# Reordering ScalarE's copies and VectorE's weight conversions in the opening of a delta-rule attention with an MLP

## The chip, the cores and the metric

The kernel runs on one core of one Trainium2 chip. A core has five engines with queues of their own, which work side by side and wait for each other through semaphores: TensorE (PE in the profile) multiplies matrices, VectorE (DVE), ScalarE (ACT) and GpSimd (POOL) work element by element, and SyncE (SP) issues most of the transfers from memory. Each engine takes its own instructions strictly in the order in which the program lists them. The metric is device microseconds for one execution; several executions are timed and their median is given.

## The reference, cut to what matters

Inputs are q, k and v (4 batches, 8 heads, 768 tokens, 48 wide), beta (one number for each token and head), and two weight matrices w_in (384 x 2048) and w_out (2048 x 384). All is float32 or float64 on the host; the weights are stored as float64.

```python
k_n = k / (norm(k) + 1e-6)
state = 0                                    # 48 x 48 for each batch and head
for t in range(S):                           # 768 tokens in order
    y[t]  = q[t] @ state
    v_old = state^T @ k_n[t]
    state = state + beta[t] * outer(k_n[t], v[t] - v_old)
x = y of all heads side by side              # 3072 x 384
h = x @ w_in
out = (h * clip(h + 3, 0, 6) / 6) @ w_out    # 3072 x 384
```

## The kernel before, in words

**Blocks of tokens.** The loop over 768 tokens is done in 24 blocks of 32 tokens, all four batches at once, so that a tile has 128 rows. I call them token blocks 0 to 23. For each block the kernel

- normalizes the keys (`norms`, `prep` at L505: the scaling is L510 on POOL);
- turns keys and queries on PE (`pt`, L524) and copies them with ACT to `KQ` (L532), keys first, then queries;
- multiplies them to scores (`sc`, L547), which DVE masks to `L` and `LB` (L558);
- needs the inverse of a triangular matrix made of `L`. Block 0 has its own product form (`product`, L569). Blocks 1 to 4 go together: `halves_of` (L715) turns `L` with L469, does a forward substitution on two half-size problems with fourteen rounds of two DVE operations (L730, L735), and turns the result back (L473). Then `join` (L666) puts the two halves together for each block, with a transposition (L694), a product on PE (`pi`, L684), an addition and a second transposition (L698, L702), a second product (L684) and a copy by ACT (L710);
- runs the `chain` (L787): read the state (`ks`, L806), form the right-hand side R (L901, L909), multiply by the inverse (`pz`, L827) and copy the result with ACT back to R (L927; for block 0 this is its only R), form the output (`py`, L827, then `y`, by ACT at L861 for block 0), turn it (`yt`, L873), copy it to `xT` (L877, ACT), and update the state (`su` on PE at L938, subtracted by DVE at L956).

**The MLP.** `up` (L982) multiplies a pair of blocks, 256 tokens, by w_in; for the first pair each block goes alone, 128 tokens. PE makes one slice of 128 hidden units at a time (`ph`, L994), ACT a scaled relu of it (L1001), DVE the gated product (L1004). I call a slice a hidden unit. A `ph` needs one of four places in PSUM; each is free again when the gated product, or the copy, that reads it is done. `down` (L1153) multiplies by w_out. From 190 us on, forms with fewer products take over; the change does not touch them.

**The weights.** They come as float64, 16 pieces of 768 KB (weights 0 to 7 are w_in, 8 to 15 w_out), and become float32 on the chip. For a piece, ACT does four steps on the exponents (`scales`, L356) and DVE three on the rest: L378, L383 (both into a buffer `m`), and L389, which multiplies the two parts into the weight's place. The exponents stand in two buffers in turn, so the first L356 of weight i must wait for the L389 of weight i - 2. A piece is loaded into a place that an earlier piece has left (L331): load 11, for example, needs the first L356 and the L383 of weight 6 done. Hidden units 1 and 2 need weight 0, units 3 and 4 weight 1, and so on.

**The order.** For the first part the order is written by hand, as a string of words, `ORDER`. Each word advances one generator by one step, so the string fixes the order in which every engine gets its instructions:

```python
gens.update(
    a=scales(), c=rest, w=pieces(), q=queries(), v=values(), B=betas(), k=keys(), z=settings(), s=more_settings(),
    ua=up(0, 0), ub=up(0, 1), u=mlp_units(),
)
makers = {
    "p": lambda t: prep(t, False), "h": lambda t: chain(t, False), "y": lambda t: outs[t],
    "n": early_norms, "m": mask, "b": scaled, "x": lambda t: product(t) if t < G0 else join(t),
    }
```

So `a` is one exponent step on ACT and `c` one conversion step on DVE; `w`, `q`, `k`, `v` are loads; `p3` is the next step of the preparation of block 3 (its steps: scale keys, turn keys, copy keys, turn queries, copy queries, scores, masks); `h0` the next of block 0's chain (product, R, update on PE, update of the state on DVE); `y0` of its output (product, y, turn, xT); `i1` one step of the substitution of blocks 1 to 4; `x1` one of block 1's join; `ua` one hidden unit of block 0, `ra` its relu, `ga` its gated product. `*n` repeats a word.

Of the kernel before, what the change touches and what calls it, by code (L numbers as in the profile page):

```python
# [22 lines left out]
k*2 B*3 k*2 n0 k*2 z B s*2 n0*6 k*2 q*2 n1 q n1 q w k p0 z*3 k n1*2 k*2 n1*2 z p0*2 s k p0*3 a k a  # L23
m0 a n2 m1 p0 x0*2 w q x0 n1 x0*3 c*2 n2 a k s p1*2 a s*2 k q s*2 x0 n2 k*2 c x0 n2 x0 w q a*4 q p1
n2 k*2 a x0 m2 p1 c*2 p1 n2*3 b1 q b0 s p1 x0 q w x0 n2 q*2 c*3 x0 n4 k p1 k p2*2 x0*2 a*2 c a*2 q*3
a*2 w v p3*2 q x0 q n4 p2*2 c p2 v c n4*2 a*3 z v n4 c a m3 v c p2 n4*2 q p2 k c b2 h0 c h0 w a*2 h0
p4*2 a*2 m4 p3 q*4 h0 q k w p4*2 c*5 v*2 p3 k p3*3 k*2 p4*2 v*2 p4 m6 k a w a w i1*3 k i1*7 a i1*2 a
i1*2 v i1*2 k b3 k y0 c y0*3 ua*2 ra*2 i1*3 w v ga v a*3 i1*2 ua i1 h1 i1 q w ua ra ua i1 ra*2 ga i1
k ua a*2 ra ga i1 ga ua ra ua ra i1 ga i1*4 ua ga n5 x1*2 k x1 c a ra v a*2 ga x2 k*2 ga*2 ua*2 x1
ra*2 x1*2 ua h1*2 n5 k ga c ra ga*2 h1 c y1*2 ua ra w ga ua ra x2 n5 ga y1*2 ua ra ga h1 v*3 n5*2 k  # L30
y1*2 ua a ra x2 ub*2 a n5 rb*2 h1 x3 ga c*2 v W a h2 y2 gb ub rb gb x2 gb ub*2 n5*2 b4 rb n5 x2*2 h2
gb rb gb m5 a n5*2 y2 ub rb gb v c q*2 v q*5 n5 ub n5 rb gb h2 c h2 q ub y2 h2 y2 rb ub p5 b5 rb
gb*2 a*2 x3 p5 ub y2*2 k p5*2 h2 rb h3 p5 gb h3 ub*2 q rb gb rb gb ub a x3 p6 v c x4 x3 rb gb ub p7
rb gb y3 c*2 v c p7*2 y3 v p7*2 b6 x3 q x3 ub p6 h3 a p6 c p5*2 rb gb k m7 w p6 h3 u p6 k*2 q*3 a*2
y3 a p6 c y3 v y3*2 u n9 v k q a c a c*2 u*2 ru gu w k a*2 c a*2 x4 c*2 ru p7 a gu k u a*2 p7 p6 m8
u*3 a k u*2 k h3 w ru*2 a*2 gu*2 x4 c*2 x4 k c*2 a p8 k a*2 u ru k h3 u*2 h4 ru a b8 gu k gu y4 p8*3
u h4 k*2 c q k*9 q u p8*2 x4 k ru k*2 gu k c n9 q u q*2 p8 k*2 b7 n9*2 i2 u x4 q i2*2 q ub ru gu u
rb gb i2*2 h4*2 u*2 i2 ru i2*6 y4 i2 gu i2*7 u i2 ru gu i2 u*3 ru i2*4 gu ru i2*2 v i2 c gu u*3 a u
ru c i2 u*2 i2 gu i2*3 q i2*5 y4 h4 n9 i2 e*2 n9*2 i2*4 q i2 y4 e n9 u ru i2*3 u i2 ru*2 gu h4 u n9
i2*2 u i2 e i2*6 y4 u k n9*3 u gu i2 y4 n9 i2 p9 q i2*2 gu  # L40
"""


# [1521 lines left out]
```

## Time and profile before

| | us |
|---|---|
| median of 3 timed runs | 663.66 (663.46 to 663.9) |
| profiled execution, its own time | 662.06 |
| span of the profiled execution | 660.3 |
| PE busy | 632.5 (96%) |
| DVE busy | 499.2 (76%) |
| ACT busy | 282.3 (43%) |
| POOL busy | 225.1 (34%) |
| PE busy in 0 to 20, 20 to 40, 40 to 60 | 7.67, 13.26, 15.57 of 20 each |

The span is what the profile covers, from the first to the last instruction; the time of the execution is a little longer. The profile gives each instruction's start and length, and in brackets how long its engine had been idle before it and which instruction let it go. Lines of the timeline put together instructions of one kind that follow each other closely ("x64"). A busy PE need not be a PE at its peak, because ends of matmuls are modelled. The granted clock (PEclk) is the share of TensorE's full clock that it was given.

### The profile page before, as it was taken

The numbers are of one execution on the slowest core, as the hardware profiler recorded it, in microseconds if no ns is written. First come the engines' busy times: TensorE is split into PE (matmuls) and PEld (weight loads), VectorE is DVE, ScalarE is ACT, GpSimd is POOL, SyncE is SP. The second block draws the span as 40 slices with busy tenths as digits, with TensorE's granted clock in tenths as the row PEclk, the third lists the DMA queues.
The fourth block names the chain that finished last, engine by engine and source line by source line (L and its number), as shares of the span: only waits on it lengthen the run. The fifth ranks groups of instructions, "written<-read, shape, count | busy, mean of one in ns | idle before, by whom it ended". The sixth has DMA issues, their size and how long they took to land.

```text
span 660.3 us, 26640 instructions
## 1 busy us (share of the span) xinstructions
PE 632.5 (96%) x11640; PEld 569.2 (86%) x11640; DVE 499.2 (76%) x1170; ACT 282.3 (43%) x548; POOL 225.1 (34%) x352
## 2 busy tenths in 40 slices
PE   2768999999999999999999999999999999999997
PEld 2658987776689989999999999999999999999997
DVE  5899877798657988758988848979658998456354
ACT  5887689332243154154154244244244144153250
POOL 6531022003661353553254354164051242331430
PEclk9998999999999999999999999999999999999999
DMA  7888346202040030041030030020020020000000
GB/s 174 204 198 235 77 102 164 51 25 43 9 87 18 3 74 3 3 90 22 3 74 3 2 74 3 2 63 2 3 50 2 3 49 3 23 18 2 26 1 24
DMA packets 88692, 33.28 MB, mean 50 GB/s; under 512 B 80224, under 2 KB 83424, under 8 KB 88576
## 3 DMA queue, kind: packets, MB, share of 16 engines
q1 hardware_dynamic: 88224, 31.29, 20.8%
q8 instruction: 91, 1.49, 0.9%
q10 hardware_dynamic: 352, 0.30, 0.2%
q14 instruction: 25, 0.20, 0.1%
HBM read 26.84 MB, written 4.72 MB: 48 GB/s over the span
## 4 chain that ended last, share of the span: by engine, by line
PE 91%; DVE 3%; DMA 2%; SPq 1%; ACT 1%; issue 1%; DVEq 0%
PE po L1226 28%; PE ph L1066 27%; PE ph L994 9%; PE po L1162 6%; PE ks L806 4%; PE su L938 3%; PE pt L524 3%; PE pz L827 3%; PE py L827 3%; PE sc L547 2%; PE yt L873 1%; DMA spare<-in_moe_w_in_dram 1%; PE pi L684 1%; DMA w_out<-in_moe_w_in_dram 1%; SPq L168 1%
## 5 line engine op out<-in xcount | busy, mean ns | idle before, releaser
L1066 PE MATMUL ph<-xT,w_in 128*128 128x128 f32 (+1 forms) x720 | 156.8, 321 | 0.0
L1030 POOL TENSOR_TENSOR g<-g 128x256 f32<-128x256 f32 (+1 forms) x144 | 88.6, 616 | 104.7 <-ACT g L1080 99.1
L1066 PEld LDWEIGHTS ph<-xT,w_in 128*128 128x128 f32 x720 | 116.8, 191 | 6.7
L1226 PE MATMUL po<-w_out,g 128*128 128x192 f32 x640 | 110.6, 326 | 0.0
L1226 PEld LDWEIGHTS po<-w_out,g 128*128 128x128 f32 x640 | 104.6, 190 | 0.5
L1080 ACT ACTIVATE g<-ph 128x512 f32<-128x512 f32 x72 | 43.1, 598 | 105.1 <-PE ph L1066 105.1
L1226 PE MATMUL po<-spare,g 128*128 128x192 f32 x480 | 86.7, 332 | 0.0
L1226 PEld LDWEIGHTS po<-spare,g 128*128 128x128 f32 x480 | 77.2, 190 | 1.8
L994 PE MATMUL ph<-xT,w_in 128*128 128x128 f32 (+1 forms) x384 | 72.0, 338 | 0.6 <-ACT xT L877 0.6
L1236 POOL TENSOR_TENSOR o<-o,u 128x192 f32<-128x192 f32 x18 | 13.3, 739 | 163.8 <-ACT o L1233 86.6
L994 PEld LDWEIGHTS ph<-xT,w_in 128*128 128x128 f32 x384 | 59.6, 195 | 7.7 <-ACT xT L877 0.8
L1093 DVE TENSOR_TENSOR g<-ph,g 128x256 f32<-128x256 f32 x72 | 30.2, 419 | 46.8 <-PE ph L1066 33.5
L759 DVE TENSOR_TENSOR pr<-A 128x30 f32<-128x30 f32 (+9 forms) x150 | 57.3, 382 | 3.3
L1212 DVE TENSOR_TENSOR g<-g 128x512 f32<-128x512 f32 x80 | 56.1, 722 | 3.5 <-PE po L1226 3.5
L1113 DVE SCALAR_TENSOR_TENSOR g<-o,g 128x512 f32<-128x512 f32 x72 | 52.6, 730 | 7.8 <-ACT o L1110 7.7
L764 DVE TENSOR_TENSOR A<-A,pr 128x30 f32<-128x30 f32 (+9 forms) x150 | 55.1, 367 | 3.3
L1110 ACT ACTIVATE o<-g,halves 128x512 f32<-128x512 f32 x72 | 52.2, 725 | 11.3 <-DVE g L1113 8.4
L1066 PE MATMUL ph<-beta_tok,sums_in 128*128 128x128 f32 x288 | 55.9, 275 | 0.0
L356 ACT ACTIVATE spare<-spare,places 128x768 uint16<-128x768 uint16 (+1 forms) x56 | 52.8, 947 | 3.2 <-DMA kf<-in_k_dram 1.6
L1233 ACT ACTIVATE o<-po 128x192 f32<-128x192 f32 x40 | 13.3, 332 | 82.7 <-PE po L1226 79.2
L510 POOL TENSOR_TENSOR kb<-kf,inv 128x384 f32<-128x384 f32 x24 | 21.7, 907 | 75.5 <-issue 43.1
L1162 PE MATMUL po<-w_out,g 128*128 128x384 f32 x128 | 45.4, 490 | 0.0
(141 smaller groups left out, 1019.1 us busy)
## 6 DMA issues: line engine op xcount, KB each, us to landing
kf<-in_k_dram SPq DMA_DIRECT2D x96, 48.0 KB, 2.6
qb<-in_q_dram SPq DMA_DIRECT2D x96, 48.0 KB, 2.4
vf<-in_v_dram SPq DMA_DIRECT2D x96, 48.0 KB, 2.1
out_dram<-o SPq DMA_DIRECT2D x90, 48.0 KB, 1.6
spare<-in_moe_w_in_dram SPq DMA_DIRECT2D x4, 768.0 KB, 6.6
w_out<-in_moe_w_in_dram SPq DMA_DIRECT2D x4, 768.0 KB, 6.1
w_out<-in_moe_w_out_dram SPq DMA_DIRECT2D x4, 768.0 KB, 5.8
spare<-in_moe_w_out_dram SPq DMA_DIRECT2D x4, 768.0 KB, 5.2
```

The source lines that it names most:

```text
L356: nc.scalar.activation(out=z, in_=z if n else d.bitcast(I16)[:, :, :, 3], func=func, bias=places[:, n : n + 1], scale=scale,)
L759: nc.vector.tensor_tensor(out=pv, in0=A[:, j + 1 :, j].unsqueeze(2).to_broadcast([n, w, j]), in1=A[:, j, 0:j].unsqueeze(1).to_broadcast([n ...
L764: nc.vector.tensor_tensor(out=A[:, j + 1 :, 0:j], in0=A[:, j + 1 :, 0:j], in1=pv, op=ALU.subtract)
L994: nc.tensor.matmul(ph[:, cols], lhsT=w_in[:, s, f * 128 : (f + 1) * 128], rhs=xT[:, s, cols], start=(s == 0), stop=(s == NKT - 1),)
L1030: nc.gpsimd.tensor_tensor(out=out, in0=a, in1=b, op=op)
L1066: nc.tensor.matmul(ph[:, n], lhsT=w, rhs=x, start=start, stop=stop, skip_group_check=True)
L1080: nc.scalar.activation(out=gt, in_=ph[:], func=ACTF.Copy)
L1110: nc.scalar.activation(out=r, in_=g, func=ACTF.Relu, bias=half, scale=1.0 / 6.0)
L1113: nc.vector.scalar_tensor_tensor(out=g, in0=r, scalar=1.0, in1=g, op0=ALU.min, op1=ALU.mult)
L1162: nc.tensor.matmul(pos[c][:], lhsT=gs[blk, f // 2][:, f % 2, c * P : (c + 1) * P], rhs=w_out[:, f, :], start=(f == 0), stop=(f == NFC - 1),)
L1212: nc.vector.tensor_tensor(out=A(f, *out, 4), in0=A(f, *a, 4), in1=A(f, *b, 4), op=op)
L1226: nc.tensor.matmul(ps[n][:], lhsT=A(f - f % 2, *a)[:, f % 2], rhs=b[:, f], start=(f == 0), stop=(f == HF - 1),)
```

## The change

Only the string `ORDER` differs. No instruction is added, removed or resized; some stand at other places in their engine's queue. The diff rewraps many lines. This is what is left when both strings are written out (the rest is the same):

```diff
 ... c p2*2 v c n4*2
-a*3 z v n4 c a m3 v c p2 n4*2 q p2 k c b2 h0 c h0 w a*2 h0 p4*2 a*2 m4
-p3 q*4 h0 q k w p4*2 c*5 v*2 p3 k p3*3 k*2 p4*2 v*2 p4 m6 k
-a w a w i1*3 k i1*7 a i1*2 a i1*2 v i1*2 k b3 k y0 c y0*3 ua*2
+a*2 z v n4 c m3 v c p2 n4*2 q p2 k c b2 h0*2 p3 a w p3*2 h0 a h0 p4*2 p3 a m4
+q*4 c p3 q k w p4*2 c p4*2 c v*2 p4 k*3 v*2 a m6 k
+y0 a y0 a*2 w a w i1*3 k i1*7 a i1*2 a i1*2 c v i1*2 k b3 k y0*2 ua*2
 ra*2 i1*3 w v ga v a*3 ...
-k ua a*2 ra ga i1 ...
+k ua a ra ga i1 ...
 ... ua ga n5 x1*2
-k x1 c a ra v a*2 ga x2 ...
+c*2 k x1 c a c a ra v a*2 ga x2 ...
```

Engine by engine, as the two programs list them:

- **ACT.** Before: the four L356 of weight 4, R of block 0 (L927), the four of weight 5, keys of blocks 3 and 4 and queries of blocks 3 and 4 (four L532), the four of weight 6, y (L861), xT (L877). After: two of weight 4, R, keys of block 3, the third, queries of block 3, the fourth, the first of weight 5, keys and queries of block 4, two of weight 5, y, the last of weight 5, the four of weight 6, xT. Later the first L356 of weight 8 goes from ahead of the relus of hidden units 6 to 8 to behind them and behind a square (L407); the relu of unit 9 stays behind it and behind the second L356 of weight 8.
- **DVE.** The last conversion of weight 4 goes behind the two updates of the state (L956). The first two of weight 5 go between the masks of block 3 and those of block 4; its third goes into the substitution, where the third of weight 6 was (one operation earlier). All three of weight 6 go behind the first transposition of block 1's join (L694), ahead of the first conversion of weight 7, of the gated products of units 7 to 9, and of L698 and L702.
- **PE.** The queries of block 3 are turned ahead of the state update of block 0, and the scores of block 3 come ahead of the turning of block 4's queries. The rest stands as before.
- **POOL and SP.** Their orders are the same.

## The prediction

> **What bounds the kernel now.** I read the page first, then busy time by stage, then the timelines of the three engines that the change reorders. The page:
>
> ```profile
> PE   2768999999999999999999999999999999999997
> PEclk9998999999999999999999999999999999999999
> ...
> PE 91%; DVE 3%; DMA 2%; SPq 1%; ACT 1%; issue 1%; DVEq 0%
> ```
>
> The chain that ended last is TensorE (PE) for 91%. In order of time nearly all its other pieces lie before 61.24 us. The stages agree:
>
> ```profile
> 40.00:60.00 20.00, 15.57 (x362) 14.15 (x354) 18.53 (x49) 16.46 (x26) 3.59 (x7) 0.91 0.89 246
> 60.00:80.00 20.00, 19.06 (x670) 17.49 (x669) 18.02 (x49) 15.53 (x36) 2.15 (x4) 1.00 0.35 99
> 80.00:100.00 20.00, 20.00 (x663) 17.23 (x663) 14.47 (x34) 15.34 (x30) 6.14 (x8) 1.00 0.45 100
> ```
>
> After the length, each group is an engine's busy time (PE, PEld, DVE, ACT, POOL). PE loses 4.4 us in 40 to 60, 0.94 in 60 to 80, and nothing more until the last slices. So the edit is worth what it moves the moment from which PE never waits again. Now that moment is the first join, at 61.24; the second join product comes at 63.43. PE's work behind it is the same in both versions.
>
> TensorE, start and length in us:
>
> ```profile
> 39.29 1.27 PE L938 MATMUL su<-R,sums_in 32*64 32x48 f32 x61 [1.75 <-ACT R L927]
> 41.31 0.44 PE L938 MATMUL su<-R,sums_in 32*64 32x48 f32 x3 [0.75 <-issue]
> 49.92 0.55 PE L873 MATMUL yt<-ident,y 128*128 128x128 f32 x3 [2.41 <-ACT y L861]
> 51.05 3.55 PE L994 MATMUL ph<-xT,w_in 128*128 128x128 f32 x18 [0.58 <-ACT xT L877]
> 61.24 0.72 PE L684 MATMUL pi<-X,sums_in 16*32 16x16 f32 x64 [0.94 <-DVE sums_in L694]
> ```
>
> ScalarE (ACT); the brackets are what the edit aims at and what it makes late:
>
> ```profile
> 38.77 0.47 ACT L927 ACTIVATE R<-pz 128x384 f32<-128x384 f32 x1
> 44.54 1.09 ACT L532 ACTIVATE KQ<-pt 128x512 f32<-128x512 f32 x2 [0.29 <-PE pt L524]
> 50.51 0.49 ACT L877 ACTIVATE xT<-yt 128x384 f32<-128x384 f32 x1 [0.64 <-PE yt L873]
> 53.35 0.37 ACT L1001 ACTIVATE g<-ph,halves 128x128 f32<-128x128 f32 x1 [0.92 <-PE ph L994]
> 56.46 0.78 ACT L1001 ACTIVATE g<-ph,halves 128x128 f32<-128x128 f32 x2
> ```
>
> VectorE (DVE), substitution start to join:
>
> ```profile
> 47.70 1.93 DVE L469 STREAM_TRANSPOSE A<-L 128x1024 f32<-128x1024 f32 x1
> 57.36 0.28 DVE L1004 SCALAR_TENSOR_TENSOR g<-g,ph 128x128 f32<-128x128 f32 x1
> 58.00 0.28 DVE L1004 SCALAR_TENSOR_TENSOR g<-g,ph 128x128 f32<-128x128 f32 x1
> 60.74 0.45 DVE L694 STREAM_TRANSPOSE sums_in<-X 128x256 f32<-128x256 f32 x1
> 61.11 0.52 DVE L378 TENSOR_SCALAR spare<-spare 128x768 uint32<-128x768 uint32 x1
> 62.54 0.44 DVE L702 STREAM_TRANSPOSE sums_in<-sums_in 128x256 f32<-128x256 f32 x1
> ```
>
> The substitution runs back to back on DVE from 47.70, with gated products (L1004) of the first hidden units between its rounds. The fifth starts at 58.00, 0.09 after its relu on ACT ended (57.91): there is no room for a later relu.
>
> **Step 1, up to the substitution.** Nothing is added or removed; work is reordered. R's copy need not queue behind two exponent steps (0.97 each): the product it reads ends at 37.53, so R runs 37.56 to 38.0 instead of 38.77 to 39.24. The update then runs from about 38.4 (one set of query transposes, 0.95, now stands ahead of it) and, with the same 0.75 issue gap, ends near 40.9 instead of 41.75. Token block 4's key transposes end at 41.9 (4 x 0.24), block 3's scores at 43.0 (1.1, as at 34.92), block 4's query transposes at 43.95; ACT copies them by 44.55; its scores end at 45.4 (0.75, as at 45.19) to 45.8 (1.18, as at 34.92). DVE has by then done two state updates, weight 4's last conversion and two of weight 5's (45.25), so it is not the limit. Two maskings, 0.35 each: the substitution starts at **46.1** instead of 47.70, a gain of 1.6.
>
> **Step 2, what ACT pays.** Between 34.96 and the copy xT, ACT has the same instructions in both (twelve exponent steps, R, four copies of keys and queries, y: about 14.8 us). Before, it idles some 0.8 among them. Now it waits 0.6 for R's product and 1.45 (42.5 to 43.95) for block 4's query transposes. y moves ahead of five exponent steps, but xT stays behind them: it starts at about 51.75, **1.2 later** than 50.51. If those waits vanish it starts at 50.3.
>
> **Step 3, the hidden wait.** PE's first hidden unit follows xT, at 52.3 instead of 51.05. First and second relu start about 53.6 and 54.9 (1.28 a unit, as 52.07 to 53.35); then, as before, three exponent steps of weight 7 (2.9) stand ahead of relus three to five, which end at 58.4, 58.75 and 59.05 (now 56.85, 57.24, 57.91). DVE, started at 46.1, reaches the third L1004 at 46.1 + 9.66 = 55.8 and waits 2.6; the fifth starts at 59.1, not 58.0. The rest (2.74 to L694's start, 0.45 for it) ends at **62.3** instead of 61.2: the gain has become a loss of 1.1.
>
> **Step 4, three conversions behind L694.** Weight 6's L378, L383 and L389 now follow L694, ahead of weight 7's L378, three L1004 and the join's L698 and L702. By 0.6, 1.05 and 0.95 (rows of weight 5, 42.26 to 44.87) that is 2.5 us on the chain to the second product. ACT adds to it: the first exponent step of weight 8 overwrites what weight 6's L389 reads, so it waits for it, and it and one more step (1.03 + 0.84) stand ahead of the ninth relu (0.37), whose L1004 is queued ahead of L698. Counted from L694's end: L389 ends at 2.5, the relu at 4.8, that L1004 at 5.05, L698 at 5.4, L702 at 5.85, PE's second product at **5.9**. Now it is 63.43 - 61.2 = 2.2. So 3.7 more.
>
> Of what is queued behind: on PE two hidden units (they fill 1.5 of the wait) and the product; behind that X's copy and the chain, which keep their distances. SP's and POOL's orders are unchanged, but load 11 (issued at 59.06) waits for weight 6's L383 and goes at about 63.9; behind it are values that now wait until 63.63 for R of the next block, which shifts with the join, and its data are first read at 95.30. That costs nothing; without cover it would be the same 4.8.
>
> **Sum:** 1.1 + 3.7 = **4.8 us**. The profiled execution took 662.06 (span 660.3, 1.76 around it); it would take 666.9. The median of the runs shown is 663.66, 1.6 above; on that I forecast **668.5**.
>
> **The clock.** PE did little from 48 to 51 and was then granted half its clock:
>
> ```profile
> 52.00:54.00 2.00, 2.00 (x12) 2.00 (x11) 1.79 (x8) 1.01 (x3) 0.00 (x0) 0.50 1.08 312
> 56.00:58.00 2.00, 2.00 (x17) 1.96 (x18) 1.89 (x10) 1.64 (x5) 0.00 (x0) 1.00 0.95 349
> ```
>
> The 18 matmuls at 51.05 took 3.55 (18 at 74.28: 2.27), the reading of the state after them 1.44 (73.20: 1.15), so such a stretch costs up to 1.6. The sum keeps this one stretch. In the new order PE is nearly idle again from 61.5 to 65.6, so a second one may follow: a rival below. The Trainium skill ("TensorE: Matmul & The Clock Gate", Part 1) states that the gate judges free-running windows of about 3.4 us and drops to half rate after an idle one. The trace agrees: 0.50 lasted from 52 to about 55.3. By that rule a second stretch is likelier than by this one case alone, which would make it some 670.
>
> **Rivals.**
> - *The waits on ACT close.* If PE runs early at its later pace (four transposes 0.60 at 82.75, 1.11 at 41.68), xT starts at 50.3 and L694 ends between 59.7 (no relu wait) and 61.2. Then -1.5 to 0, plus 3.7: 2.2 to 3.7, **666.6** in the middle. For it: PE has fewer gaps ahead. Against it: its transposes are slow throughout 18 to 44.
> - *The clock falls twice.* The scores and outputs of step 1 stay at the slow pace (0.8 on xT) and a second half-rate stretch follows the join (up to 1.6): 4.8 + 0.8 to 2.4, **670.3**.
> - *Half of it.* No relu wait, and the ninth relu is no wait either: -1.5 + 2.5 = +1.0, **664.7**, within 0.2%.
> - *Faster.* The earlier substitution carries through to the join and the conversions behind L694 fall into slots that nobody waits for: -1.6, **662.1**. It decides from where L702 ends ahead of 63.4; with L694 at 59.7 that leaves 3.7 for a queue that I count at 5.85. I see no row that shortens it so.
> - *It does not do what it says:* block 4's scores wait for its transposes in PE's queue anyway, and the substitution starts at 47.4. L694 is held by the relus, so the sum stays near 4.8; it is part of the forecast.
>
> **How the numbers follow.** Forecast 0.50 (667.6 to 669.6), closed waits 0.20, clock twice 0.16, half 0.08, faster 0.06. A measurement of this kernel tells 0.2% (1.3 us) from no change. Slower 0.86, same 0.08, faster 0.06. The range leaves out "half", "faster" and the ends of the others: 665.5 to 671.0.
>
> **What would show it.** Step 1: L469 starts near 46.1 (47.4 or more: wrong). Step 2: xT starts at 51 to 52. Step 3: a wait of DVE for ACT ahead of the third L1004, some 2 us, and L694 ending after 61.2. Step 4: PE waits twice between the first join product and the second, which starts about 6 us behind L694; ACT waits for DVE ahead of weight 8. Then PE full to the end. The forecast is wrong if PE waits after 75 us in the new kernel, or if the ninth relu does not stand in the join's way.

## The result and the profile after

| | before | after |
|---|---|---|
| median, 6 runs each on one chip (us) | 663.53 (662.48 to 663.9) | 670.19 (667.24 to 674.01) |
| profiled execution, its span (us) | 662.06, 660.3 | 670.92, 669.1 |

The ratio is 1.0105, with a 95% interval of 1.0071 to 1.0139: the change makes the kernel slower by 6.7 us. In the profiled executions it is 8.9 us; of the kernel after that one lies 0.7 above its median, and of the kernel before 1.5 below. The steps below are read in the profiled ones.

The page of the kernel after, where the fourth slice of PE and the granted clock of the third to the fifth are lower than before and nothing later is (the record of the clock of the kernel before begins only at 45 us, in the third slice; see the last section):

```profile
PE   2766999999999999999999999999999999999997
PEclk9967899999999999999999999999999999999999
...
PE 92%; DMA 2%; DVE 1%; SPq 1%; ACT 1%; issue 1%
```

Busy time by stage (length, then PE, PEld, DVE, ACT, POOL, granted clock, DMA share, GB/s):

```profile
40.00:60.00 20.00, 12.74 (x293) 10.72 (x294) 13.75 (x37) 12.90 (x19) 2.29 (x6) 0.57 0.96 237
60.00:80.00 20.00, 16.54 (x451) 15.32 (x454) 15.66 (x39) 11.60 (x26) 2.15 (x4) 0.83 0.24 60
80.00:100.00 20.00, 20.00 (x650) 18.61 (x640) 16.49 (x45) 14.93 (x33) 4.50 (x6) 1.00 0.38 86
```

PE loses 7.3 us in 40 to 60, where it lost 4.4, and 3.5 in 60 to 80, where it lost 0.94. From 80 us on it is full. So the loss lies ahead of the moment from which PE no longer waits; that moment is now the second join product (71.15 us; behind 75 us PE waits only once, for 0.2). PE in the kernel after:

```profile
38.02 1.17 PE L938 MATMUL su<-R,sums_in 32*64 32x48 f32 x57
40.85 0.33 PE L938 MATMUL su<-R,sums_in 32*64 32x48 f32 x7 [1.66 <-issue]
46.34 0.48 PE L547 MATMUL sc<-KQ 64*32 64x64 f32 x17 [0.90 <-issue]
53.83 4.21 PE L994 MATMUL ph<-xT,w_in 128*128 128x128 f32 x18 [4.07 <-ACT xT L877]
65.08 0.73 PE L684 MATMUL pi<-X,sums_in 16*32 16x16 f32 x64 [0.97 <-DVE sums_in L694]
68.30 2.93 PE L994 MATMUL ph<-xT,w_in 128*128 128x128 f32 x12 [2.49 <-DVE g L1004]
71.15 1.05 PE L684 MATMUL pi<-X,sums_in 32*32 32x16 f32 x64
```

"issue" means that PE stood still and no semaphore that the profile shows held it. It did so inside the state update and again inside block 4's scores. The waits for ACT (4.07) and DVE (2.49) are those of the prediction. ACT and DVE:

```profile
37.11 0.49 ACT L927 ACTIVATE R<-pz 128x384 f32<-128x384 f32 x1 [0.97 <-PE pz L827]
48.31 0.49 ACT L861 ACTIVATE y<-py 128x384 f32<-128x384 f32 x1 [2.09 <-PE py L827]
53.31 0.47 ACT L877 ACTIVATE xT<-yt 128x384 f32<-128x384 f32 x1
67.49 1.00 ACT L356 ACTIVATE spare<-w_out,places 128x768 uint16<-128x768 int16 x1 [3.23 <-DVE w_in L389]
69.36 0.35 ACT L1001 ACTIVATE g<-ph,halves 128x128 f32<-128x128 f32 x1
```

```profile
47.66 1.94 DVE L469 STREAM_TRANSPOSE A<-L 128x1024 f32<-128x1024 f32 x1
60.26 0.29 DVE L1004 SCALAR_TENSOR_TENSOR g<-g,ph 128x128 f32<-128x128 f32 x1 [2.41 <-ACT g L1001]
64.59 0.44 DVE L694 STREAM_TRANSPOSE sums_in<-X 128x256 f32<-128x256 f32 x1
66.49 0.96 DVE L389 SCALAR_TENSOR_TENSOR w_in<-spare 128x768 f32<-128x768 f32 x1
70.33 0.45 DVE L702 STREAM_TRANSPOSE sums_in<-sums_in 128x256 f32<-128x256 f32 x1
```

R is 1.66 us earlier than before (37.11, was 38.77), and yet the substitution (L469) starts at 47.66, where it was 47.70. xT is 2.8 later, L694 ends 3.84 later (65.03, was 61.19), and the second product stands 6.12 behind that end, where it was 2.24. From that product to the end of the span it is 597.95 us, where it was 596.9. 3.84 + 3.88 + 1.05 = 8.8, which is the whole difference of the spans.

### The profile page after: what moved, and what is told of

Same layout as the page of the kernel before. It is cut to its first block, busy times and chain, and to the rows that moved or that the text cites. A ratio compares the mean times of both kernels' runs of the same rounds, so it can differ in the third digit from the quotient of the medians.

```text
span 669.1 us, 26639 instructions
## 1 busy us (share of the span) xinstructions
PE 636.4 (95%) x11640; PEld 571.9 (85%) x11640; DVE 499.3 (75%) x1170; ACT 281.2 (42%) x548; POOL 224.0 (33%) x352
## 3 DMA queue, kind: packets, MB, share of 16 engines
q8 instruction: 91, 1.49, 0.9%
## 4 chain that ended last, share of the span: by engine, by line
PE 92%; DMA 2%; DVE 1%; SPq 1%; ACT 1%; issue 1%
PE po L1226 28%; PE ph L1066 27%; PE ph L994 10%; PE po L1162 6%; PE ks L806 4%; PE pt L524 3%; PE py L827 3%; PE pz L827 3%; PE su L938 3%; PE sc L547 3%; PE yt L873 1%; DMA w_out<-in_moe_w_in_dram 1%; SPq L168 1%; DMA spare<-in_moe_w_in_dram 1%; PE pi L684 1%
## 5 line engine op out<-in xcount | busy, mean ns | idle before, releaser
L1066 PE MATMUL ph<-xT,w_in 128*128 128x128 f32 (+1 forms) x720 | 156.8, 321 | 0.0
L1066 PEld LDWEIGHTS ph<-xT,w_in 128*128 128x128 f32 x720 | 116.9, 191 | 6.6
L994 PE MATMUL ph<-xT,w_in 128*128 128x128 f32 (+1 forms) x384 | 74.6, 347 | 6.8 <-ACT xT L877 4.1
L994 PEld LDWEIGHTS ph<-xT,w_in 128*128 128x128 f32 x384 | 61.9, 203 | 14.4 <-ACT xT L877 4.5
L356 ACT ACTIVATE spare<-spare,places 128x768 uint16<-128x768 uint16 (+1 forms) x56 | 52.3, 941 | 2.8 <-DMA kf<-in_k_dram 1.7
L1162 PE MATMUL po<-w_out,g 128*128 128x384 f32 x128 | 45.4, 490 | 0.0
```

Source lines behind the costliest of these rows:

```text
L356: nc.scalar.activation(out=z, in_=z if n else d.bitcast(I16)[:, :, :, 3], func=func, bias=places[:, n : n + 1], scale=scale,)
L994: nc.tensor.matmul(ph[:, cols], lhsT=w_in[:, s, f * 128 : (f + 1) * 128], rhs=xT[:, s, cols], start=(s == 0), stop=(s == NKT - 1),)
L1066: nc.tensor.matmul(ph[:, n], lhsT=w, rhs=x, start=start, stop=stop, skip_group_check=True)
L1162: nc.tensor.matmul(pos[c][:], lhsT=gs[blk, f // 2][:, f % 2, c * P : (c + 1) * P], rhs=w_out[:, f, :], start=(f == 0), stop=(f == NFC - 1),)
```

## The experiments

The edits are given as words of `ORDER` or as lines of code. The table has the profiled execution of each kernel (us; distance: from L694's end to the second join product) and the ratio of its runs to those of the kernel before on the same chip.

| kernel | L469 starts | xT starts | L694 ends | distance | ratio (95%) |
|---|---|---|---|---|---|
| before | 47.70 | 50.51 | 61.19 | 2.24 | |
| after | 47.66 | 53.31 | 65.03 | 6.12 | 1.0105 (1.0071 to 1.0139) |
| after_again | 47.15 | 52.86 | 63.84 | 5.80 | 1.0084 (1.0052 to 1.0116) |
| e1 | 48.90 | 53.97 | 65.04 | 2.44 | 1.0044 (1.002 to 1.0069) |
| e2 | 47.33 | 50.09 | 60.89 | 6.12 | 1.0059 (1.0039 to 1.0079) |
| e3 | 48.08 | 50.22 | 61.91 | 6.14 | 1.006 (1.0037 to 1.0083) |
| e4 | 47.21 | 52.26 | 63.76 | 6.13 | 1.0097 (1.0072 to 1.0122) |
| e5 | 48.05 | 53.69 | 65.44 | 6.13 | 1.0115 (1.0073 to 1.0157) |
| e6 | 48.14 | 53.81 | 63.25 | 5.81 | 1.0228 (1.0192 to 1.0264) |
| e7 | 47.81 | 53.48 | 64.37 | 4.81 | 1.0221 (1.0181 to 1.026) |
| e8 | 48.57 | 50.71 | 64.45 | 3.90 | 1.0027 (1.0009 to 1.0045) |
| e9 | 49.52 | 55.22 | 66.00 | 5.93 | 1.0194 (1.0166 to 1.0221) |
| e10 | 44.44 | 51.38 | 63.18 | 6.13 | 1.019 (1.0142 to 1.0238) |
| e11 | 48.50 | 51.36 | 62.19 | 2.24 | 1.0135 (1.0093 to 1.0178) |

**e1: the three conversions in the substitution instead of behind L694** (the kernel after, changed).

```diff
-k ua a ra ga i1 ...
-c*2 k x1 c a c a ra v a*2 ga x2
+k ua a ra c*3 ga i1 ...
+k x1 a c a ra v a*2 ga x2
```

> The changed kernel with one thing else: weight 6's three conversions stand ahead of the third gated product in the substitution, where VectorE idles 2.4 us in the changed kernel waiting for a relu, and no longer behind L694. My theory (late relus hold L694, and the conversions behind it lengthen the way to the second join product): L694 ends at about the same place as in the changed kernel (65.0, give or take 0.5), ScalarE no longer waits for weight 6 ahead of weight 8, and the second join product starts 2.3 to 2.6 us behind L694's end instead of 6.1; the time falls by 3.5 to 5 us from the changed kernel, to 665 to 667. Rival (the loss is the slow clock and the issue gaps ahead of the substitution, and the order behind L694 matters little): within 1.5 us of the changed kernel.

Measured: the conversions ran while DVE waited for the third relu, L694 ended at 65.04 as in the kernel after, and the second product came 2.44 behind it. PE of e1, with no wait between the two join products:

```profile
65.10 0.73 PE L684 MATMUL pi<-X,sums_in 16*32 16x16 f32 x64 [0.99 <-DVE sums_in L694]
65.75 1.60 PE L994 MATMUL ph<-xT,w_in 128*128 128x128 f32 x12
67.48 0.72 PE L684 MATMUL pi<-X,sums_in 32*32 32x16 f32 x64
```

So the conversions' place is worth 3.7 us here, and DVE's wait was real: three conversions fitted into it at no cost.

**e2: the conversions behind L694 alone** (the kernel before, changed: weight 6's conversions and the first step of weight 8 go where the change has them).

```diff
-... p4 c*5 v*2 p3 ... k y0 c y0*3 ... k ua a*2 ra ga ... x1*2 k x1 c a ra
+... p4 c*3 v*2 p3 ... k y0 y0*3 ... k ua a ra ga ... x1*2 c*2 k x1 c a c a ra
```

> The kernel before with the third part alone: weight 6's three conversions go behind L694, and the first exponent step of weight 8 behind the square, which it has to follow. My theory: substitution starts 0.3 earlier (47.4, the scores of block 4 end at 46.7), but its fifth gated product still waits for a relu that ends at 57.9, so L694 still ends near 61.2; the second join product starts 5.9 us behind it instead of 2.2: 3.7 us slower than before, 667.2, up to 1.6 more if TensorE then gets a second stretch at half clock. Rival (the conversions behind L694 fall into slots that nobody waits for): L694 ends 1.2 to 2.5 earlier and the kernel is faster than before by 1 to 2 us.

Measured: 667.84 us. L694 ended 0.3 earlier, no more; the relus hold it, not by the fifth as I expected but by the third, which DVE waited 0.77 for. The second product came at 67.01, 3.6 later than before. PE of e2:

```profile
64.15 2.93 PE L994 MATMUL ph<-xT,w_in 128*128 128x128 f32 x12 [2.49 <-DVE g L1004]
67.01 0.80 PE L684 MATMUL pi<-X,sums_in 32*32 32x16 f32 x64
```

This part alone makes 3.9 of the 6.7 us. It is the same price as in e1, taken from the other side.

**e3: xT ahead of the exponent steps** (the kernel after, changed).

```diff
-y0 a y0 a*2 w a w i1*3 ... k b3 k y0*2 ua*2
+y0 a y0 a y0*2 a w a w i1*3 ... k b3 k ua*2
```

> The changed kernel with one thing else: block 0's y is turned and copied to xT ahead of weight 6's four exponent steps instead of behind them. My theory: xT starts near 49.8 instead of 53.3, the first relu waits only for the four exponent steps (54), the third ends near 57.5 instead of 60.2, L694 ends at 61 to 62 instead of 65.0, and the way from there to the second join product stays at about 6: 3 to 4 us less than the changed kernel, 666 to 667. Rival (the substitution is late for itself, by the scores that come late): L694 within 1 us of 65.0 and the time within 1 us of the changed kernel.

Measured: xT at 50.22, no wait of 2.4 for the third relu, and L694 ended at 61.91, 3.1 earlier, although the substitution itself started 0.4 later. So xT's place in ACT's queue, through the relus, is what made L694 late. The distance stayed at 6.14, and the time (668.10 us) improved by less than L694 did and less than expected: the granted clock was 0.50 from 64.5 to 74.7 (the 12 matmuls after the second wait took 2.93; from the second product to the end it was 600.65, where the kernel after has 597.95).

**e4: the ninth relu ahead of the first step of weight 8** (the kernel after, changed).

```diff
-c*2 k x1 c a c a ra
+c*2 k x1 c ra a c a
```

> The changed kernel with one thing else: the ninth relu stands ahead of weight 8's first two exponent steps. My theory: VectorE no longer waits 1.3 us for it ahead of L698, and the second join product starts about 4.7 us behind L694's end instead of 6.1; weight 8's steps then stand ahead of X's copy, so that about 1 us is left as a gain. If the 6.1 us come from VectorE's own queue and the clock, nothing changes.

Measured: a miss. The distance stayed at 6.13. L702 ended early, but PE was not ready:

```profile
67.03 2.93 PE L994 MATMUL ph<-xT,w_in 128*128 128x128 f32 x12 [2.49 <-DVE g L1004]
69.89 1.05 PE L684 MATMUL pi<-X,sums_in 32*32 32x16 f32 x64
```

The two hidden units ahead of the product ran at half clock, 2.93 where e1 shows 1.60. They and the ninth relu are two equally long ways.

**e5: the load of weight 6 later** (the kernel after, changed).

```diff
-q*4 c p3 q k w p4*2 c p4*2 c v*2 p4 k*3 v*2 a
+q*4 c p3 q k p4*2 c p4*2 c v*2 p4 k*3 v*2 w a
```

PE's stop inside the update fell where transfers fill the DMA engines; this takes one of them away.

> The changed kernel with one thing else: the load of weight 6 (768 KB) is issued behind seven smaller loads, near 42.5 instead of 37.24. It tells why the substitution did not start 1.6 us earlier. In all five kernels so far TensorE stops inside block 0's state update for a reason that the profile doesn't show, and goes on at 40.6 to 41.7 whether the update began at 37.3 or at 39.3. Theory: what it waits for there comes over the same 16 DMA engines as the loads, and the load of weight 6 holds it up; then it goes on 1 to 3 us earlier, the scores of block 4 end by 45 and L469 starts 1 us or more earlier, though the time falls by less than 1 us because the relus hold L694. Rival (the stop is not the loads' doing): it ends at 40.6 to 41.7 again.

Measured: the load was issued at 42.95, and still the stop was 2.41 long and ended at 41.66. PE also stopped for 1.24 up to 35.69, as e3 did for 0.70; of the places in the table, none moved by more than the kernel after moves between its two profiles. That load is not what PE waits for.

**e6 and e7: matmuls that only keep PE busy** (the kernel after, and e4, each with 15 transposes of the identity behind block 0's `yt` and 18 behind the first join product, whose tile is made larger for them).

```diff
+            if t == 0:
+                ring("pc", NPC, ("warm", t))
+                spin = psC.tile([128, 2, 512], FP32, name="spin", tag=slot["pc"])
+                for _ in range(15):
+                    nc.tensor.transpose(spin[:, 0, 0:P], ident[:], ident[:])
+                read(("warm", t))
...
+            if t == 1 and name == "pi1":
+                for _ in range(18):
+                    nc.tensor.transpose(whole[:, 2], ident[:], ident[:])
```

> The changed kernel with TensorE kept busy in its two long gaps: 15 transpositions of the identity that nobody reads behind block 0's yt, 18 behind the first join product (the PSUM tile of that product is made larger for them). Clock theory (part of the loss is that TensorE, left idle, gets half its clock just when the joins need it): granted clock near 1.0 from 54 to 80, the first three hidden units take 2.3 us instead of 4.2, the two units ahead of the second join product 1.6 instead of 2.9; L694 ends about 1 us earlier, the second product starts 5.8 us behind it (now held by the ninth relu) and what follows gains another 1: 2 to 3 us less than the changed kernel, near 667.5. Rival (the clock changes nothing, the waits for ScalarE and VectorE set the time): within 1 us of the changed kernel.

> The one with the ninth relu ahead of weight 8, with the same 33 idle transpositions. There the second join product still came 6.1 us behind L694, because the two hidden units ahead of it ran at half clock. If the two ways to it (the ninth relu over ScalarE; the units at half clock on TensorE) were equally long, taking away both shortens it to 4.7 to 5.0 us, and the time falls 1 us or so below that of the kernel with the idle transpositions alone: 666 to 667. If VectorE's own queue holds it, it stays at 5.8.

Measured: behind the join the clock stayed up in both, and the two units took 1.60. With that alone (e6) the distance was 5.81, held by the ninth relu; with both (e7) 4.81. The 15 behind `yt` kept the clock up for the first three units in e6 (2.27, was 4.21), but not in e7 (4.15). The times are a miss: both were 9 to 10 us slower than the kernel after. The waits of PE of e6 after 75 us, where the kernel after has a single one of 0.2 (total, times, longest):

```profile
PE sc L547 <- issue: 3.2, 2, 2.7
PE py L831 <- issue: 1.7, 1, 1.7
PE su L948 <- issue: 1.4, 1, 1.4
```

New stops of the same kind as in the update, in a stage where nothing was edited. So the 33 matmuls cost far more than the 5.3 us that they kept PE busy in e6, and these times say nothing on the clock; only the rows do.

**e8: e1 and e3 together**, the best of what was found.

> The changed kernel with two of the single changes together: xT ahead of weight 6's exponent steps, and weight 6's conversions in the substitution. My theory of two causes in a row: xT first takes 2.5 us of relu wait away, so the conversions no longer fall into an empty slot there and push L694 by about 2.2; L694 ends near 64, the second join product 2.4 behind it (66.5), some 1 us better than with the conversions alone (1.0044 of before) and not the sum of both savings: 1.002 to 1.004. If the two savings simply add up, it is at 1.000 to 1.001.

Measured: 665.99 us (12 runs), 1.0027 of before. The savings don't add: the conversions in front of the third gated product made PE wait 1.86 for a place in PSUM, the clock fell, and the distance was 3.90 instead of 2.44.

**e9: eight more matmuls ahead of the update** (the kernel after; they write unused columns of block 2's score tile).

```diff
+        if t == 2:
+            for _ in range(8):
+                nc.tensor.transpose(sc[:, 0, 256:384], ident[:], ident[:])
```

> The changed kernel with 8 transpositions of the identity, read by nobody, ahead of block 2's scores, in unused columns of their PSUM tile. It asks what the stop in block 0's state update hangs on. If on a place in TensorE's instruction stream, it comes 8 matmuls earlier in the update: behind its 49th instead of its 57th. If on a wait of the update itself, it stays behind the 57th. Either way the time moves by less than 2 us from the changed kernel (the 8 cost up to 1.9 where TensorE waits 0.7 anyway).

Measured: the stop came after the 49th matmul of the update, not the 57th, and lasted 4.74 us:

```profile
37.60 0.83 PE L941 MATMUL su<-R,sums_in 32*64 32x48 f32 x49
43.18 0.49 PE L941 MATMUL su<-R,sums_in 32*64 32x48 f32 x15 [4.74 <-issue]
```

So it lies at a fixed place of TensorE's instruction stream, counted in instructions: in 12 of the 14 profiles PE stops behind its 729th matmul from the start, whichever that is. The page names a queue for instructions (queue: packets, MB, share); this is the kernel after:

```profile
q8 instruction: 91, 1.49, 0.9%
```

A packet has 16 KB. 1.49 MB over PE's 11640 matmuls and 11640 weight loads is 64 bytes for each, so a packet holds about 128 matmuls with their loads; between the two stops of the kernel after there are 7 + 4 + 64 + 4 + 47 = 126 matmuls. In the 14 profiles PE made 40 stops of over 0.25 us marked "issue" between 10 and 140 us. Set against the packets of that queue in the trace, each ended 1.25 to 1.84 us after the latest packet had landed (kernel before: landed 39.81, PE went on at 41.31; after: 39.39 and 40.85, 44.93 and 46.34; e9: 41.57 and 43.18).

**e10 and e11: 48 matmuls fewer in the update**, in the kernel after and in the kernel before. Both leave out most heads' own keys there, so the state is no longer that of the reference; they serve the timing alone.

```diff
-            for p in range(NP):
+            n = NP if t == 0 else 1
+            for p in range(0, NP, n):
...
-                            su[b // 2][DP * e : DP * e + DP, b % 2, D * p : D * p + D],
-                            lhsT=bkb[rows(b), h], rhs=Z[rows(b), D * h : D * h + D],
+                            su[b // 2][DP * e : DP * e + DP, b % 2, D * p : D * p + D * n],
+                            lhsT=bkb[rows(b), h], rhs=Z[rows(b), D * h : D * h + D * n],
```

> The changed kernel with one edit: the state update of block 0 multiplies four heads at once by one head's keys, so that it takes 16 matmuls where it took 64; the state it writes is that of wrong keys. Theory A, the stop lies at a fixed place of TensorE's instruction stream because the instructions arrive in packets there (every stop of the runs so far ended 1.25 to 1.85 us after a packet of the instruction queue had landed, and consecutive stops are some 126 matmuls apart, 40.85 and 46.34 in the changed kernel): with 48 matmuls fewer the first place moves out of the update into the scores of block 3, still at about 40.9, and the second moves behind block 4's scores. Then only 27 scores, 4 transposes, a copy and 64 scores stand behind the first stop: block 4's scores end at 43.6 to 44.3 without a stop, and the substitution starts at 44.5 to 45.3 instead of 47.66; xT at 50.0 to 51.1, the first transposition of the join ends at 62.1 to 62.8, the second join product starts at 68.2 to 68.9, ratio 1.005 to 1.008. Theory B, the stop belongs to the update itself or to a moment: it stays inside the update or at its end, up to about 40.9, block 4's scores stop again, and the substitution starts at 46.8 or later; ratio 1.009 or more.

> The kernel before with the same edit (block 0's update in 16 matmuls, wrong keys for most heads). Theory A: no stop in the update; block 4's scores end up to 0.5 us earlier than 46.70, but VectorE (conversions to 46.46 and four masks of 0.35) and ScalarE (four copies behind exponent steps that end at 43.3) hold the substitution: it starts at 47.1 to 47.5 instead of 47.70, and the time stays within 0.2% of before. So with the packets out of the way the change's order starts the substitution 2 to 3 us earlier than the order before, as my first step meant, where with 64 matmuls it gains nothing. Theory B: the substitution starts within 0.3 us of 47.70 too, and the distance between the two orders stays under 1 us.

Measured in e10 (PE): the stop moved into block 3's scores, 28 matmuls ahead of their end, up to 41.03; block 4's scores ran through, and the next stop is in `py`:

```profile
39.70 0.60 PE L547 MATMUL sc<-KQ 64*32 64x64 f32 x36 [0.54 <-DVE state L957]
41.03 0.45 PE L547 MATMUL sc<-KQ 64*32 64x64 f32 x28 [0.73 <-issue]
42.75 0.86 PE L547 MATMUL sc<-KQ 64*32 64x64 f32 x64 [0.69 <-ACT KQ L532]
45.78 0.55 PE L827 MATMUL py<-R,LB 32*32 32x48 f32 x33 [1.70 <-issue]
```

The substitution started at 44.44, 3.2 earlier than in the kernel after, just ahead of the expected 44.5 to 45.3. Not all of it is the stops': block 4's scores end 3.2 earlier (43.61, were 46.82), and 1.0 of that is the clock, which was full from 37.6 to 47.8 here (0.46 on the four transposes ahead of them, 0.58 on the scores). The other 2.2 go with the moved places. xT was a little later than expected (51.38), because the second stop holds y. Both ratios were a miss, as in e6: new stops after 75 us (3.9 in all in e10, one of 2.0). In e11 the substitution came later than expected, 48.50, because DVE waited 1.01 for the data of weight 6. The two orders then lie 4.1 us apart, where with 64 matmuls they lie level; 1 of it is that wait, and some of it the clock, since e11 ran the 128 scores in 2.06 (1.51 in the kernel before).

**after_again: the kernel after once more**, beside e5 to e7.

> The changed kernel once more, beside the three others on the same chip, as their measure: 1.007 to 1.014 of the time before, if the first measurement holds.

Measured: 670.46 us. Its profile had one stop, up to 40.84, and the scores of block 4 without one, but PE reached their 48th matmul, where the kernel after has its second one, only at 45.83; L469 started at 47.15. Between its two profiles the kernel after moves by 0.5 us at L469 and by 1.2 at the end of L694; smaller differences at these two places say nothing.

## Why the prediction was right in part

**Step 1 failed.** It let "the update ... end near 40.9", block 4's scores at 45.4 to 45.8 and the substitution start at 46.1. The update did end at 41.2, but not as foreseen: it began 0.4 early, and its stop lasted 1.66 instead of 0.75. Block 3's scores ended at 42.75 and the copy of block 4's queries at 44.43 (foreseen 44.55). Then block 4's scores took 2.34 us instead of 0.75 to 1.18: a stop of 0.90, and half clock. The rival "it does not do what it says" (47.4) came true, for another reason than it gave. What stood in the way is the arrival of PE's instructions: they come in packets of some 127 matmuls, and in this stage PE could go on with the next one only at 40.85 and 46.34, whatever was ready. In the kernel before PE came to the same second place at 46.3 and did not notice. In the second profile of the kernel after the first place alone held it (2.01, up to 40.84); half clock behind that (four transposes 1.11, scores 1.18 to 1.19 for 64) was then enough for 47.15. An order that makes data ready earlier gains nothing at such a place; e10, which moves the places, gets the earlier substitution, 2.2 us of it by the places and 1.0 by the clock. I took the row with 0.75 "issue" in the kernel before for a fixed cost of the update; it was the sign of this limit.

**Step 2 was right in kind, mis-sized:** xT at 53.31, not 51.75. The missing 1.6 are block 4's late scores and `py` at half clock (1.50, was 0.88), which y waited 2.09 for. The five exponent steps then stood between y and xT as foreseen; e3 shows what they cost.

**Step 3 held:** the relus set L694, and DVE waited 2.41 for the third of them. That this is so near to my 2.6 is luck: the substitution started 1.6 later than I had it, and the third relu ended 1.8 later. L694 ended at 65.03, not 62.3: 1.56 from xT, and 1.15 because the first three units (4.21, was 3.55) and the reading of the state (1.93, was 1.44) ran wholly at half clock.

**Step 4 held:** distance 6.12, foreseen 5.9; e1 and e2 show it from both sides. The ninth relu is only half of what stands in the join's way. The two hidden units on PE, which I let fill 1.5, take 2.93 at half clock and are as late: PE waited once between the two products, not twice as I had it. e4 and e6 each took one of the two away and gained 0 to 0.3, e7 took both and gained 1.3.

**The clock fell twice** behind step 1, a rival. The granted clock was 0.50 from 42.7 to 59.7 and from 66.6 to 73.4; the second stretch begins here:

```profile
66.00:68.00 2.00, 0.00 (x0) 0.00 (x0) 1.93 (x4) 0.51 (x1) 0.00 (x0) 0.64 0.39 39
68.00:70.00 2.00, 1.70 (x8) 1.71 (x9) 0.70 (x5) 1.97 (x4) 0.00 (x0) 0.50 0.81 324
```

PE did nothing from 66 to 68, and behind it the units ran at half clock. Behind the second product this cost 1.05 (the product 1.05, was 0.73, and what followed). The Trainium skill ("TensorE: Matmul & The Clock Gate", Part 1) has windows of about 3.4 us for this; the trace agrees, the stretches being 17.07 and 6.83 us, five and two times 3.41. The rule spoke for a second stretch, and it came. But it speaks of an idle window, and these were not: in the 3.41 us that ended with each of the two falls PE was busy 1.67 and 1.69.

**The sum.** Foreseen 4.8; in the profiled execution 8.9: 2.7 more at L694 (step 1 and the clock), 0.2 more in step 4, 1.05 for the second stretch. The median rose by 6.7, to 670.2. That this is the 670.3 of the rival with two stretches is in part luck: its own terms give 669.3 to 670.9 on the median and at most 7.2 us, the profiled execution lost 8.9, and its 0.8 on xT was 1.56 and held a stop that it did not know. The likeliest case, with an earlier substitution and one stretch, is not what happened. Nor can a measurement tell 0.2%, as I wrote: the six runs of the kernel after lie 1% apart, and the interval of the ratio is 0.34% to either side.

**What stays open:** why the instruction packets come so late here. Between 26 and 46 us they start 5.6 to 5.8 us after each other in the kernel after, while the DMA engines carry weights and inputs (mean share 0.80); between 85 and 102 us 3.5 to 4.6 (0.34). That the transfers hold them up is only argued; the one load that was moved (e5) was not it. Against it, a packet's own transfer takes little longer there (0.96 to 1.43 us, and 0.92 to 1.18 later); what is late is its start. The four in question start when PE has begun 400, 536, 672 and 808 matmuls, nearly a packet apart, so PE's own progress may set off the next one; but in the kernel before it is 428, 536, 668 and 740. No run separates the two. Nor was a longer lead of the packets tried. That the stops also caused the half clock, by leaving PE idle for 1.66, fits the rows but was not tried by itself.

## What to carry to other kernels

Before crediting an earlier operand, look for "issue" waits in the stage behind it: a stop without a releaser can be a limit that the new order runs into, not a cost that stays. Work moved into a queue is paid where that queue ends last, so look for the wait on the same engine into which it fits free of charge (e1), rather than for a place that looks idle in the share of busy time. And a gap of PE of 2.5 us cost twice here, once by itself and once at half clock behind it.

## What the runs showed of the hardware

TensorE's instruction supply was a limit in this kernel: stops of 0.3 to 4.7 us at places some 127 matmuls apart, each ended 1.25 to 1.84 us after a 16 KB packet of the instruction queue had landed. Small matmuls (64 in 0.7 to 1.2 us) use up a packet in some 1.4 to 2.4 us by that count, where packets came 5.6 to 5.8 us apart. Adding 8 or 33 matmuls to the opening, or taking 48 away, moves other matmuls to these places, and made the kernel slower by 6 to 10 us each time. New stops are a good part of that (6.3 us behind 75 us in e6, 3.9 in e10); the rest is not accounted for.

A granted clock of 1.00 ahead of the first entry of a trace's record is no measurement. The kernel before shows 1.00 up to 51.8, but its record has no entry ahead of 44.98, and its four transposes took 1.11 at 41.68. The kernel after, whose trace has changes from 32.4 on, shows 0.50 up to 39.3 with transposes of 1.05 and 1.11, and 1.00 from there to 42.7 with 0.66. So the kernel before most likely ran at half clock too until 44.98, just ahead of its fast scores (128 in 1.51, from 45.19); and the drop of the clock's share from 0.91 to 0.57 in 40 to 60 is in part the record's. I had taken the slow transposes for their size at full clock.

How idle PE has to be for the clock to fall can be read from the 14 traces. The clock changes in steps of 3.41 us. Up to 140 us it fell 37 times, each time at the end of such a step in which PE was busy for 57% or less of it; it stayed full only behind steps with 52% or more. It rose 37 times, each time behind a step with 86% or more. So about half a step's work was the border for keeping it up here, and it took nearly a full one to bring it back.
